# Attention, convolution block and gated block on one core: batch 0 turns its probabilities on TensorE, and the first layer's products stay in PSUM through relu, taps and gate

## The chip, the cores and the metric

The kernel runs on one core of one Trainium2 chip. The metric is device microseconds of that core, the median of three runs: 476.09 us before the change (474.88 to 476.97). Engines are named as the profile names them: PE is TensorE, PEld its weight loads, DVE is VectorE, ACT is ScalarE, POOL is GpSimd, SP is SyncE, which issues all DMAs of this kernel from one queue, in order.

## What is computed

Three layers in a row on 4 batches of 576 positions. The first is causal attention in a window of 128 keys with a linear bias, 8 heads of 64. The second multiplies by `w_in` (512 to 1024), takes relu, forms a gate from 3 taps along the sequence, and multiplies by `w_out` (1024 to 512). The third forms a gate from 5 taps on its input, multiplies the input by `w_val`, gates it and multiplies by `w_out2`.

```python
scores = np.where(mask, scale * q @ k.T + bias, -1e9)
attn = softmax(scores)
x = attn @ v
h = np.maximum(x @ w_in, 0.0)
conv = sum(conv_w[k] * hp[:, k:k + S] for k in range(3))
y = (h * sigmoid(conv)) @ w_out
gate_pre = sum(conv_w2[k] * yp[:, k:k + S] for k in range(5))
out = (sigmoid(gate_pre) * (y @ w_val)) @ w_out2
```

All arrays are float32 in the reference's sense, but the weights and `cw` reach the chip as 64-bit floats and are widened from their two halves on the chip.

## The kernel before, in words

The sequence of each batch is cut into two units, u = 0 (positions 0 to 254, with 256 columns in the first layer) and u = 1 (the rest, with 328 columns). So there are 8 units, (b, u). Each goes through `hidden` (w_in, relu, 3 taps, gate), `mixed` (w_out, 5 taps), `valued` (w_val) and `output` (w_out2). While a unit runs through these four, the attention of the next one is mixed in: four head pairs, each with 4 query blocks of 64 (u = 0) or 5 (u = 1).

The order of all instructions comes from a planner inside the program (`Program.forward` and `backward`): every operation is added with an engine or a choice of engines, an estimated duration, what it reads and writes, and a priority; a list scheduler lays them on the engines, repeats this seven times with priorities from the pass before, and keeps its shortest plan. The engines then run that order, each strictly in its own. Buffers are rings; an operation waits for the last reader of its buffer.

**Attention of one pair** (`attention`): a DMA brings q and k (L502), another v (L505). Scores go to a PSUM bank (`pss`, 3 banks, 2 for the first 20 uses), two blocks to a bank (L541, float32 matmuls). DVE adds the bias and finds the minimum (L545), ACT takes the exponential in place in PSUM with its sum (L549), POOL or DVE and then DVE make the reciprocal `st` (L554, L552, L559). ACT writes the scaled probabilities as float16 to `p` (L575, the high part), DVE the rest (L577, the low part). There is one `p` buffer. When all blocks of a pair are written, SP issues two DMA transposes from `p` to `pt` (L585), one for each part; then PE multiplies by v into `psx` (L617), from where ACT and DVE make the two parts of x (L633, L638, L640).

**Products.** Every weight and every activation is held as a high and a low part, and a product is three matmuls (L657, L658, L659). `dense` takes a bank of the ring `pm` (4 banks, 2 for the first 16 uses, because the widening of the weights uses the other two).

**hidden**, for each of 8 blocks of 128 channels: 12 matmuls into a `pm` bank, then ACT writes the relu to a buffer of ring `t` in SBUF (L692) and so frees the bank. The middle tap goes to a second `t` buffer, on ACT or DVE (L344, L345); two more taps are added by DVE (`fma`, L351), in two of the 8 blocks one of them by ACT and POOL (L361, L362). ACT takes tanh (L702), DVE forms the gate times h (L703, recorded at L351 as `t<-t,t`), and ACT or POOL makes the high part (L335, L337), POOL the low one (L366).

**Weights** (`widen`): a DMA brings a chunk of 512 KB to `raw` (3 buffers, L387), ACT moves its upper word twice (L388 to SBUF, L390 to PSUM), DVE joins the words (L392, L401), ACT or POOL makes the high part (L407, L408), POOL the low part (L366). There are 24 chunks, 8 each of w_in and w_out, 4 each of w_val and w_out2.

**Start.** Until the attention of unit (1, 0), PE is given matmuls on a zero tile wherever its plan is empty (`warm`, L817). DVE instructions that read or write only SBUF, and POOL's, are marked `port=True`: the planner makes them longer where the two run at once.

## Time and profile before

| what | value |
|---|---|
| median of three runs | 476.09 us (474.88 to 476.97) |
| the profiled execution, its own time | 474.43 us |
| its span, first to last instruction | 472.6 us |
| PE, PEld busy (share of the span) | 94%, 88% |
| DVE, ACT, POOL busy | 80%, 71%, 54% |
| mean granted TensorE clock | 0.993 |

Busy times are unions of an engine's instruction records. A matmul record spans its pipeline, so a busy PE is not a PE at its peak. The line after `<-` in a row names what ended the idle time before it. A line number can be that of a helper: L351 is `fma`, L344 and L345 `scaled`, L335 and L337 `cast`, L366 `sub`.

### The profile page before, as it was taken

To read this page: it belongs to the slowest core of one execution; us is meant where nothing else is said; L and a number is where in the kernel's file an instruction comes from. 1 tells how busy PE (TensorE), PEld (TensorE's weight loads), DVE (VectorE), ACT (ScalarE), POOL (GpSimd) and SP (SyncE) were. 2 spreads that over 40 slices of the span, in tenths; PEclk is the share of its full clock that TensorE was granted. 3 is DMA by queue.
4 is the path that set the end of the run, shared out by engine and by line. 5 is a ranking of instruction groups with operands and counts; after the bars stand their busy time and mean duration, and the time that the engine had idled before them with its cause. 6 is when DMAs were issued, how large, how long until landed. Compare 5 with 4: busy or idle time off the path is not lost.

```text
span 472.6 us, 10284 instructions
## 1 busy us (share of the span) xinstructions
PE 446.6 (94%) x3568; PEld 414.0 (88%) x3568; DVE 377.7 (80%) x1009; ACT 334.7 (71%) x964; POOL 256.6 (54%) x379
## 2 busy tenths in 40 slices
PE   7998988879999899999999999999999999999996
PEld 5776876878999899998989899999989999989895
DVE  4688998799898949995999668966999489927690
ACT  3788978898675658785966778765766687846542
POOL 1445987887366607450467447441874167735542
PEclk9999999889999999999999999999999999999999
DMA  8998869699824244646324634666144626640001
GB/s 269 193 235 253 233 149 291 182 236 264 244 59 117 71 118 99 144 102 158 94 47 120 129 94 110 123 145 157 31 98 87 151 64 146 100 101 1 1 0 57
DMA packets 93156, 62.32 MB, mean 132 GB/s; under 512 B 73904, under 2 KB 83888, under 8 KB 93104
## 3 DMA queue, kind: packets, MB, share of 16 engines
q1 hardware_dynamic: 93104, 61.67, 52.4%
q8 instruction: 28, 0.46, 0.4%
q14 instruction: 24, 0.20, 0.1%
HBM read 39.10 MB, written 4.72 MB: 93 GB/s over the span
## 4 chain that ended last, share of the span: by engine, by line
DVE 33%; PE 23%; ACT 9%; issue 6%; POOL 4%; DMA 1%; ACTq 0%; POOLq 0%
DVE t L351 13%; DVE gts L351 10%; PE pm L657 6%; PE pm L658 6%; PE pm L659 6%; PE pss L541 3%; PE psx L617 3%; POOL g L366 2%; DVE p L577 2%; ACT pss L549 2%; DVE pss L545 2%; ACT p L575 1%; ACT t L344 1%; DMA vr<-in_vN 1%; DVE v L351 1%
## 5 line engine op out<-in xcount | busy, mean ns | idle before, releaser
L366 POOL TENSOR_TENSOR g<-t,g 128x254 fp32r<-128x254 f32 (+1 forms) x96 | 85.9, 901 | 18.0 <-ACT g L335 14.2
L351 DVE SCALAR_TENSOR_TENSOR t<-t,cc,t 128x326 f32<-128x326 f32 (+3 forms) x112 | 77.5, 713 | 11.7 <-ACT t L344 10.8
L657 PE MATMUL pm<-g,wout 128*128 128x254 f32 (+1 forms) x256 | 81.1, 317 | 2.0 <-ACT t L344 1.8
L549 ACT ACTIVATE pss<-pss,st 128x192 f32<-128x192 f32 (+2 forms) x144 | 53.9, 374 | 38.0 <-DVE st L545 31.3
L351 DVE SCALAR_TENSOR_TENSOR gts<-t,cc,gts 128x322 f32<-128x322 f32 (+4 forms) x120 | 76.6, 676 | 4.7 <-ACT gts L344 4.0
L657 PE MATMUL pm<-x,win 128*128 128x256 f32 (+1 forms) x256 | 78.7, 307 | 0.0
L658 PE MATMUL pm<-g,wout 128*128 128x254 f32 (+1 forms) x256 | 77.3, 302 | 1.2 <-POOL g L366 1.1
L659 PE MATMUL pm<-g,wout 128*128 128x254 f32 (+1 forms) x256 | 76.8, 300 | 0.8 <-POOL wout L366 0.7
L659 PE MATMUL pm<-x,win 128*128 128x256 f32 (+1 forms) x256 | 76.0, 297 | 0.3 <-POOL win L366 0.3
L658 PE MATMUL pm<-x,win 128*128 128x256 f32 (+1 forms) x256 | 76.2, 298 | 0.0
L541 PE MATMUL pss<-qk 128*128 128x192 f32 (+2 forms) x288 | 57.5, 325 | 7.9 <-DVE p L577 7.8
L554 POOL TENSOR_SCALAR st<-st 128x2 f32<-128x2 f32 (+1 forms) x66 | 16.0, 242 | 85.3 <-ACT pss L549 82.5
L545 DVE CUSTOM_DVE_ANT_0 pss<-pss,bm 128x192 f32<-128x192 f32 (+2 forms) x144 | 47.7, 342 | 14.1 <-PE pss L541 12.6
L337 POOL TENSOR_SCALAR g<-t 128x254 fp32r<-128x254 f32 (+1 forms) x53 | 28.3, 536 | 52.9 <-DVE t L351 36.4
L577 DVE SCALAR_TENSOR_TENSOR p<-pss,st,p 128x192 f16<-128x192 f32 (+2 forms) x139 | 48.8, 387 | 9.8 <-ACT p L575 9.3
L541 PEld LDWEIGHTS pss<-qk 128*128 128x128 f32 x288 | 44.2, 192 | 12.6 <-DVE p L577 11.7
L575 ACT ACTIVATE p<-pss,st 128x192 f16<-128x192 f32 (+2 forms) x139 | 49.2, 404 | 4.8 <-DVE st L559 2.1
L657 PEld LDWEIGHTS pm<-g,wout 128*128 128x128 f32 x256 | 49.0, 191 | 3.6 <-ACT t L344 2.0
L658 PEld LDWEIGHTS pm<-g,wout 128*128 128x128 f32 x256 | 49.3, 193 | 2.0 <-POOL g L366 2.0
L659 PEld LDWEIGHTS pm<-g,wout 128*128 128x128 f32 x256 | 49.3, 193 | 1.2 <-POOL wout L366 1.2
L657 PEld LDWEIGHTS pm<-x,win 128*128 128x128 f32 x256 | 48.3, 189 | 1.5 <-issue 0.9
L659 PEld LDWEIGHTS pm<-x,win 128*128 128x128 f32 x256 | 48.2, 188 | 0.5 <-POOL win L366 0.5
(100 smaller groups left out, 1169.9 us busy)
## 6 DMA issues: line engine op xcount, KB each, us to landing
qk<-in_qk SPq DMA_DIRECT2D x16, 544.0 KB, 4.1
qk<-in_qk SPq DMA_DIRECT2D x16, 384.0 KB, 3.8
raw<-in_w_out SPq DMA_DIRECT2D x12, 512.0 KB, 4.2
raw<-in_w_in SPq DMA_DIRECT2D x8, 512.0 KB, 5.4
vr<-in_vN SPq DMA_DIRECT2D x16, 256.0 KB, 2.9
raw<-in_vN SPq DMA_DIRECT2D x8, 384.0 KB, 3.8
out<-t SPq DMA_DIRECT2D x16, 161.0 KB, 1.9
raw<-in_w_val SPq DMA_DIRECT2D x4, 512.0 KB, 3.9
```

The costliest lines, as they stand in the source:

```text
L337: "POOL": (pool_t(n), lambda: nc.gpsimd.tensor_scalar(hi, src, 1.0, 0.0, op0=ALU.mult, op1=ALU.add))}
L351: pg.add("DVE", dve_t(n, 0 if isinstance(scalar, float) else 1), lambda: nc.vector.scalar_tensor_tensor(out=out, in0=in0, scalar=scalar, i ...
L366: "POOL": (pool_t(n, True), lambda: nc.gpsimd.tensor_tensor(out=lo, in0=src, in1=hi.bitcast(F32), op=ALU.subtract))}
L541: return [nc.tensor.matmul(out=o, lhsT=q_t[:, i, :], rhs=k_t[:, kc:kc + nkey], start=True, stop=True, skip_group_check=True) for i, o, nke ...
L545: pg.add("DVE", 128 + 1.05 * nkey, lambda i=i, s=s, nkey=nkey: nc.vector.tensor_tensor_reduce(out=s, in0=s, in1=bm[:, p, 192 - nkey:192], ...
L549: pg.add("ACT", act_t(nkey, True, 2), lambda i=i, s=s: nc.scalar.activation(out=s, in_=s, func=AF.Exp, scale=-1.0, bias=stt[:, 0, i:i + 1] ...
L554: "POOL": (165, lambda a=a, e=e: nc.gpsimd.tensor_scalar(stt[:, 2, a:e], stt[:, 1, a:e], 1e-9, 1.0 / PSC, op0=ALU.add, op1=ALU.mult))}
L575: pg.add("ACT", act_t(nkey, True, 1), lambda i=i, s=s, hi=hi: nc.scalar.activation(out=hi, in_=s, func=AF.Copy, scale=stt[:, 2, i:i + 1]), ...
L577: pg.add("DVE", dve_t(nkey, 1), lambda i=i, s=s, hi=hi, lo=lo: nc.vector.scalar_tensor_tensor(out=lo, in0=s, scalar=stt[:, 2, i:i + 1], in ...
L657: return [nc.tensor.matmul(out=o, lhsT=wh, rhs=hi, start=first, stop=False), nc.tensor.matmul(out=o, lhsT=wh, rhs=lo, start=False, stop=Fa ...
L658: nc.tensor.matmul(out=o, lhsT=wh, rhs=lo, start=False, stop=False),
L659: nc.tensor.matmul(out=o, lhsT=wl, rhs=hi, start=False, stop=last)]
```

## The change

In batch 0 (`b < TURN`), ACT writes the exponential unscaled, as float32, to the `p` buffer, which holds the same bytes seen as 10 x 128 floats. For each query block a diagonal matrix `dg` = identity times the reciprocal is made by DVE or POOL (ring of 3). PE multiplies: the probabilities are the stationary operand, `dg` the moving one, so that PSUM receives the transposed and scaled probabilities, in the bank that held the scores. There are 64 such matmuls of 128 columns: 6 for a pair of u = 0, 10 for one of u = 1. ACT copies them as float16 to `pt` (high part), DVE subtracts for the low part, one instruction each for a group of one or two query blocks. The 16 DMA transposes of batch 0 are gone; batches 1 to 3 are as before. The zeroes in `p` are set again for float16 before batch 1.

In `hidden`, in all batches, the relu is written in place in the `pm` bank. The middle tap, the other two and the gate read it there, so the bank is released by the gate and not by the relu. Ring `t` has 9 buffers in place of 10. The planner's cost of a transfer is scaled by 1.17 and not by 1.3, and that of a transposed block goes from 142 to 162 before scaling, which leaves a transpose where it was and makes other transfers cheaper in its eyes.

```diff
+TURN = 1
...
-    ring_t = Ring("t", 10, [128, XMAX], F32)
+    ring_t = Ring("t", 9, [128, XMAX], F32)
...
+    ring_dg = Ring("dg", 3, [128, 128], F32)
...
-        return pg.add("SP", issue, fn, prio, reads, writes, 0.0, xfer * 1.3)
+        return pg.add("SP", issue, fn, prio, reads, writes, 0.0, xfer * 1.17)
...
+        turn = b < TURN
+        pe_ = pb.rearrange("p q a c -> p (q a c)").bitcast(F32)
...
+                if turn:
+                    c0 = 256 * i + 128 * (j0 + i < 2) + 64 * ((j0 + i) % 2 and j0 + i > 1)
+                    to, tok = pe_[:, c0:c0 + nkey], ((pk, 0, i),)
...
+                    pg.add(("DVE", "POOL"), (dve_t(128, 1, True), pool_t(128, False, 1)), (
+                        lambda dg=dg, ri=ri: nc.vector.tensor_scalar(dg, eye, ri, None, op0=ALU.mult),
+                        lambda dg=dg, ri=ri: nc.gpsimd.tensor_scalar(dg, eye, ri, 0.0, op0=ALU.mult, op1=ALU.add)),
+                        pr, ((stk, 2, gi), "eye"), (dk,), port=True)
...
+                        return [nc.tensor.matmul(out=gp[:, 128 * (x - 2 * a):128 * (x - 2 * a) + 128], lhsT=pe_[:, 128 * x:128 * x + 128],
+                                                 rhs=dg, start=True, stop=True, skip_group_check=True) for x in sl]
+                    pg.add("PE", len(sl) * mm4_t(128), rows, pr, ((pk, 0, i), dk), ((sk, 0), (sk, 1)))
...
+                pg.add("ACT", act_t(128 * sn, True), lambda src=src, hi=hi: nc.scalar.activation(out=hi, in_=src, func=AF.Copy),
+                       pr, ((sk, 0), (sk, 1)), ((ptk, 0, gi),), bank=sk)
+                pg.add("DVE", dve_t(128 * sn), lambda src=src, hi=hi, lo=lo: nc.vector.tensor_tensor(
+                    out=lo, in0=src, in1=hi, op=ALU.subtract), pr, ((sk, 0), (sk, 1), (ptk, 0, gi)), ((ptk, 1, gi),), bank=sk)
+                continue
...
-        for q in range(2):
+        for q in range(0 if turn else 2):
...
-            h, hk2 = ring_t.next()
...
+            h = hp
+            pg.add("ACT", act_t(Nx, True), lambda h=h: nc.scalar.activation(out=h[:, 0:Nx], in_=h[:, 0:Nx], func=AF.Relu),
+                   pr, (), (hk,), bank=hk)
+            scaled(c, h[:, d:d + Ng], c1[:, m, 1:2], Ng, pr, (hk, "cc"), (ak,), ('ACT', 'DVE'), True, hk)
...
-            fma(c, c, 1.0, h[:, d:d + Ng], ALU.add, ALU.mult, Ng, pr, (hk2,), (ak,))
+            fma(c, c, 1.0, h[:, d:d + Ng], ALU.add, ALU.mult, Ng, pr, (hk,), (ak,), hk)
```

How the order moves is shown at three places. The first is SP's queue near the start, from the first chunk of w_in on (`raw` receives weights, `qk` queries and keys, `vr` values). Before:

```order
L387 DMA raw1_75<-in_w_in 128x1024
L502 DMA qk0_106<-in_qk0 128x768
L585 DMA_TRANSPOSE pt0_117<-p0_116 128x7x128 x2
L387 DMA raw0_74<-in_cw 128x88
L387 DMA raw2_76<-in_w_in 128x1024
L502 DMA qk1_107<-in_qk0 128x768
L585 DMA_TRANSPOSE pt1_118<-p0_116 128x7x128 x2
L387 DMA raw0_74<-in_w_in 128x1024
L502 DMA qk0_106<-in_qk1 128x1088
L585 DMA_TRANSPOSE pt0_117<-p0_116 128x7x128 x2
L387 DMA raw1_75<-in_w_in 128x1024
```

Now:

```order
L389 DMA raw1_75<-in_w_in 128x1024
L389 DMA raw0_74<-in_cw 128x88
L389 DMA raw2_76<-in_w_in 128x1024
L504 DMA qk0_105<-in_qk0 128x768
L507 DMA vr0_107<-in_vN 128x512
L504 DMA qk1_106<-in_qk0 128x768
L389 DMA raw0_74<-in_w_in 128x1024
L389 DMA raw1_75<-in_w_in 128x1024
L389 DMA raw2_76<-in_w_in 128x1024
L504 DMA qk0_105<-in_qk1 128x1088
```

No load stands behind a transpose any more until batch 1; loads wait for free buffers alone.

The second place is PE at the second pair of unit (0, 0) (`pss0` and `pss1` are score banks). Before, the scores of the second pair follow zero matmuls, and nothing but scores is in the banks:

```order
L541 MATMUL pss0_123<-qk1_107 128x64
L541 MATMUL pss0_123<-qk1_107 128x128
L817 LDWEIGHTS idle_73
L817 MATMUL pss2_125<-idle_73 128x256
L817 LDWEIGHTS idle_73
```

Now the turned probabilities of the first pair are made just ahead of these scores:

```order
L585 MATMUL pss1_126<-dg2_118,p0_115 128x128 x2
L585 MATMUL pss1_126<-dg0_116,p0_115 128x128 x2
L547 MATMUL pss0_125<-qk1_106 128x64
L547 MATMUL pss0_125<-qk1_106 128x128
L858 LDWEIGHTS idle_73
```

Six matmuls with `dg` have come in for this pair (two for its first bank stand further up). In the whole program the zero matmuls go from 284 to 173.

The third place is DVE in `hidden` of unit (0, 1) (`t` are SBUF buffers, `pm` PSUM banks, `cc` the taps). Before:

```order
L351 SCALAR_TENSOR_TENSOR t5_100<-t4_99,cc_69,t5_100 128x326
L345 TENSOR_SCALAR t7_102<-t6_101,cc_69 128x326
L351 SCALAR_TENSOR_TENSOR t5_100<-t4_99,cc_69,t5_100 128x325
L351 SCALAR_TENSOR_TENSOR t7_102<-t6_101,cc_69,t7_102 128x326
L351 SCALAR_TENSOR_TENSOR t5_100<-t5_100,t4_99 128x326
```

Now:

```order
L353 SCALAR_TENSOR_TENSOR t0_95<-pm3_124,cc_69,t0_95 128x326
L353 SCALAR_TENSOR_TENSOR t8_103<-pm2_123,cc_69,t8_103 128x325
L353 SCALAR_TENSOR_TENSOR t0_95<-pm3_124,cc_69,t0_95 128x325
L551 ISA pss1_126,st1_114<-pss1_126,bm_72 128x64
L551 ISA st1_114 128x1
L353 SCALAR_TENSOR_TENSOR t8_103<-t8_103,pm2_123 128x326
```

One of the two wide operands of every tap and gate is now a PSUM bank. In the whole program DVE's middle taps of `hidden` (L345, now L347) go from 13 to 25.

## Rows read from the trace of the kernel before

**Rows 1.** Stretches: length, busy PE, PEld, DVE, ACT, POOL, clock, DMA share, GB/s.
```profile
0.00:40.00 40.00, 33.81 (x273) 26.09 (x273) 27.41 (x98) 28.15 (x87) 15.33 (x35) 1.00 0.93 232
40.00:80.00 40.00, 36.22 (x313) 31.12 (x313) 38.18 (x96) 34.63 (x92) 31.90 (x42) 1.00 0.80 232
80.00:118.00 38.00, 31.84 (x256) 29.09 (x255) 34.00 (x87) 33.62 (x92) 31.62 (x39) 0.91 0.84 227
118.00:472.00 354.00, 344.78 (x2733) 327.73 (x2731) 278.14 (x731) 238.29 (x699) 177.71 (x264) 1.00 0.42 99
```

**Rows 2.** PE's waits from 118 to 472 us: total, times, longest.
```profile
PE pm L658 <- POOL g L366: 3.4, 7, 0.8
```

**Rows 3.** Stretches with two transposes and little else, columns as in rows 1.
```profile
150.50:153.50 3.00, 2.86 (x25) 2.56 (x24) 2.96 (x3) 1.81 (x5) 3.00 (x4) 1.00 0.82 153
194.40:198.00 3.60, 3.60 (x30) 3.60 (x29) 3.60 (x6) 1.99 (x5) 2.25 (x4) 1.00 0.99 182
```

**Rows 4.** SP's timeline: the fourth pair's transposes, the last w_in chunk.
```profile
31.70 2.72 SPq L585 DMA_TRANSPOSE pt<-p  x2
...
38.88 0.33 SPq L387 DMA_DIRECT2D raw<-in_w_in  x1
```

**Rows 5.** PE's timeline: PE begins w_in in earnest; later one run of scores.
```profile
40.35 0.38 PE L657 MATMUL pm<-x,win 128*128 128x256 f32 x1
...
221.99 2.01 PE L541 MATMUL pss<-qk 128*128 128x192 f32 x12
```

**Rows 6.** DVE's groups by shape, 0 to 118 us: count, busy us, mean ns, idle.
```profile
L392 DVE SCALAR_TENSOR_TENSOR pm<-pm,sg 128x512 uint32<-128x512 uint32 x24 | 16.8, 699 | 3.2 <-ACT pm L390 3.0
...
L577 DVE SCALAR_TENSOR_TENSOR p<-pss,st,p 128x192 f16<-128x192 f32 x31 | 11.5, 408 | 0.2
...
L351 DVE SCALAR_TENSOR_TENSOR t<-t,t 128x254 f32<-128x254 f32 x8 | 6.5, 823 | 0.0
...
L351 DVE SCALAR_TENSOR_TENSOR t<-t,cc,t 128x254 f32<-128x254 f32 x8 | 6.2, 793 | 0.0
L351 DVE SCALAR_TENSOR_TENSOR t<-t,cc,t 128x253 f32<-128x253 f32 x6 | 4.3, 709 | 0.0
...
L742 DVE SCALAR_TENSOR_TENSOR gts<-gts,pm 128x254 f32<-128x254 f32 x4 | 1.6, 404 | 0.0
...
L345 DVE TENSOR_SCALAR t<-t,cc 128x254 f32<-128x254 f32 x1 | 0.3, 334 | 0.0
```

**Rows 7.** DVE's timeline: a tap, then two gates one after the other.
```profile
62.28 0.47 DVE L351 SCALAR_TENSOR_TENSOR t<-t,cc,t 128x254 f32<-128x254 f32 x1
...
62.95 0.41 DVE L351 SCALAR_TENSOR_TENSOR t<-t,t 128x254 f32<-128x254 f32 x1
...
63.36 1.42 DVE L351 SCALAR_TENSOR_TENSOR t<-t,t 128x254 f32<-128x254 f32 x1
```

**Rows 8.** ACT's and POOL's groups by shape, 0 to 118 us, columns as in rows 6.
```profile
L390 ACT ACTIVATE pm<-raw 128x512 f32<-128x512 f32 x24 | 15.4, 641 | 0.0
...
L575 ACT ACTIVATE p<-pss,st 128x192 f16<-128x192 f32 x31 | 11.6, 419 | 0.9 <-DVE st L559 0.8
...
L337 POOL TENSOR_SCALAR g<-t 128x254 fp32r<-128x254 f32 x7 | 3.3, 478 | 0.4 <-DVE t L351 0.4
```

**Rows 9.** Timelines, hidden of unit (0, 1): first and fourth relu, their gates, a matmul.
```profile
121.75 0.45 ACT L692 ACTIVATE t<-pm 128x328 f32<-128x328 f32 x1 [2.06 <-PE pm L659]
...
126.94 0.43 ACT L692 ACTIVATE t<-pm 128x328 f32<-128x328 f32 x1
...
124.91 0.95 DVE L351 SCALAR_TENSOR_TENSOR t<-t,t 128x326 f32<-128x326 f32 x1
...
133.03 0.49 DVE L351 SCALAR_TENSOR_TENSOR t<-t,t 128x326 f32<-128x326 f32 x1
...
126.26 0.32 PE L658 MATMUL pm<-x,win 128*128 128x328 f32 x1
126.42 0.31 PE L659 MATMUL pm<-x,win 128*128 128x328 f32 x1
```

More of the change, by code (lines that the diff above doesn't have):

```diff
@@ L339, in cast, with scaled @@
         pg.add(use, tuple(engs[e][0] for e in use), tuple(engs[e][1] for e in use), prio, reads, writes, port=True)
-    def scaled(out, in_, scale, n, prio, reads, writes, engs, psum=False):
+    def scaled(out, in_, scale, n, prio, reads, writes, engs, psum=False, bank=None):
         ap = 0 if isinstance(scale, float) else 1
@@ L347, in scaled, with fma, tap @@
         pg.add(tuple(engs), tuple(how[e][0] for e in engs), tuple(how[e][1] for e in engs), prio, reads, writes,
-               port=not psum)
-    def fma(out, in0, scalar, in1, op0, op1, n, prio, reads, writes):
+               bank=bank, port=not psum)
+    def fma(out, in0, scalar, in1, op0, op1, n, prio, reads, writes, bank=None):
         pg.add("DVE", dve_t(n, 0 if isinstance(scalar, float) else 1), lambda: nc.vector.scalar_tensor_tensor(
-            out=out, in0=in0, scalar=scalar, in1=in1, op0=op0, op1=op1), prio, reads, writes, port=True)
-    def tap(out, in0, w, n, prio, reads, key, shared):
+            out=out, in0=in0, scalar=scalar, in1=in1, op0=op0, op1=op1), prio, reads, writes, bank=bank, port=bank is None)
+    def tap(out, in0, w, n, prio, reads, key, shared, bank=None):
         if not shared:
-            fma(out, in0, w, out, ALU.mult, ALU.add, n, prio, reads, (key,))
+            fma(out, in0, w, out, ALU.mult, ALU.add, n, prio, reads, (key,), bank)
             return
@@ L360, in tap @@
         t = t[:, 0:in0.shape[1]]
-        pg.add("ACT", act_t(n, False, 1), lambda: nc.scalar.activation(out=t, in_=in0, func=AF.Copy, scale=w), prio, reads, (tk,))
+        pg.add("ACT", act_t(n, bank is not None, 1), lambda: nc.scalar.activation(out=t, in_=in0, func=AF.Copy, scale=w), prio, reads, (tk,), bank=bank)
         pg.add("POOL", pool_t(n, True), lambda: nc.gpsimd.tensor_tensor(out=out, in0=out, in1=t, op=ALU.add), prio, (tk,), (key,))
@@ L580, in attention @@
         ca, ce = (1, 8) if u == 0 else (0, 10)
-        pt, ptk = ring_pt.next()
         pr = prio + step * nb
-        for q in range(2):
+        if not turn:
+            pt, ptk = ring_pt.next()
+        for q in range(0 if turn else 2):
             src = pb[:, q, ca:ce, :].rearrange("p a c -> p (a c)")
             sync(lambda q=q, src=src: nc.sync.dma_start_transpose(out=pt[:, q, ca:ce, :], in_=src),
-                 pr, tuple((pk, q, i) for i in range(nb)), ((ptk, q),), (ce - ca) * 142.0, 650.0)
+                 pr, tuple((pk, q, i) for i in range(nb)), tuple((ptk, q, gi) for gi in range(3)), (ce - ca) * 162.0, 650.0)
         if u == 0:
@@ L624, in attention @@
             dur = sum(64 * m[5] * m[7] / 2.4 + 27 for _, m in ms if m[-1] == 0) + 7
-            rd = tuple((ptk, q) for q in sorted({g[0] for g in gr})) + tuple((vk, q + 1) for q in sorted({g[1] for g in gr}))
+            rd = tuple((ptk, q, gi) for q in sorted({g[0] for g in gr}) for gi in range(len(groups))) + tuple((vk, q + 1) for q in sorted({g[1] for g in gr}))
             pg.add("PE", dur, lambda ms=ms: do_pv(ms), pr, rd, (xpk,)).drain = True
@@ L691, in hidden @@
             c = a[:, 0:Ng]
-            how = {"ACT": (act_t(Nx, True), lambda h=h, hp=hp: nc.scalar.activation(out=h[:, 0:Nx], in_=hp[:, 0:Nx], func=AF.Relu)),
-                   "DVE": (dve_t(Nx), lambda h=h, hp=hp: nc.vector.tensor_scalar(h[:, 0:Nx], hp[:, 0:Nx], 0.0, None, op0=ALU.max))}
-            use = ('ACT',)
-            pg.add(use, tuple(how[x][0] for x in use), tuple(how[x][1] for x in use), pr, (hk,), (hk2,))
-            scaled(c, h[:, d:d + Ng], c1[:, m, 1:2], Ng, pr, (hk2, "cc"), (ak,), ('ACT', 'DVE'))
+            h = hp
+            pg.add("ACT", act_t(Nx, True), lambda h=h: nc.scalar.activation(out=h[:, 0:Nx], in_=h[:, 0:Nx], func=AF.Relu),
+                   pr, (), (hk,), bank=hk)
+            scaled(c, h[:, d:d + Ng], c1[:, m, 1:2], Ng, pr, (hk, "cc"), (ak,), ('ACT', 'DVE'), True, hk)
             for i, k in enumerate((0, 2)):
@@ L810, in attention_moe_moe_kernel @@
             if u2 == 0:
+                if b2 == TURN:
+                    zeros(False, base)
                 prepare(b2, base - 10000)
```

38 lines of the change are left out of this document (28 added, 10 removed).

## The prediction, made before the changed kernel was run

> **What bounds the kernel now.** I read the table of stretches first, then PE's waits, then the queue, the groups of DVE and the timeline of one `hidden` stage.
>
> The stretches [rows 1] show two regimes. From 118 us on PE is busy 344.8 of 354 us, while DVE has 278.1, ACT 238.3 and the DMA share is 0.42. The waits that the view can name there are small: the longest entry for PE is 3.4 us, on POOL's low part of an activation [rows 2]. So after 118 us time goes only if PE is given less to do, and what can be won from waits is a few us. Before 118 us it is different. In the first 40 us the DMA share is 0.93, DVE is busy 27.4 us and ACT 28.2 us: the chip is waiting for data and for the attention's chain. From 40 to 118 us DVE is busy 38.2 + 34.0 = 72.2 of 78 us, 93%, with ACT at 34.6 + 33.6 = 68.2 us: the vector work of widening, attention and `hidden` sets the pace. PE is not the bound there: 284 of its matmuls are the zero ones, all before 118 us. So I cost the change as: how much earlier does PE get into its saturated stretch, and what does it then find changed.
>
> **Start, 0 to 40 us.** A pair of transposes of u = 0 takes 0.82 x 3.0 = 2.5 us of all DMA engines, one of u = 1 0.99 x 3.6 = 3.6 us [rows 3]. The four pairs of unit (0, 0) are thus 9.8 of the 37 us of DMA work in this stretch. They are also obstacles in SP's queue: the fourth pair's is issued at 31.70 us and the last chunk of w_in at 38.88 us [rows 4], and PE begins the run of w_in at 40.35 us [rows 5]. In the new order no load stands behind one. The gain lies between 0, if the attention's chain on DVE and ACT sets the 40 us anyway, and 9.8 us. In the chain the transposes' landing is replaced by a diagonal, two to four matmuls, a copy and a subtraction. I take 7 us, nearer the upper end, because DVE is idle 12.6 us and ACT 11.8 us of these 40.
>
> **DVE, 40 to 118 us.** Removed: 36 low parts of batch 0 at 0.408 us for 192 columns [rows 6] (28 of them, and 8 shorter ones, estimated at 0.31), 13.9 us. Added: 12 subtractions over 512 columns, at most 0.699 us as the widening's PSUM instruction of that width, and 8 over 256 at 0.404 us as the gating of `valued` [rows 6], 11.6 us; and 13 diagonals of 128 columns, at about 0.334 us, the middle tap from SBUF [rows 6], 4.3 us. That is +2.0 us. In `hidden` of unit (0, 0) the 8 gates took 0.823 us and the 14 taps 0.793 and 0.709 us: 6.6 + 6.3 + 4.3 = 17.2 us [rows 6]. They are long because something holds them: the same gate takes 0.41 us once and 1.42 us right after, a tap 0.47 us [rows 7]. An instruction with one operand in PSUM, L742, has a mean of 0.404 us [rows 6]. From PSUM I take 0.404 for a gate and 0.47 for a tap: 9.8 us, a gain of 7.4. Three more middle taps go to DVE, 3 x 0.47 = 1.4 us. Sum -4.0 us, and at 93% busy -4.3 us of time. The bounds are +3.7 us (no gain from PSUM) and -7 us (subtractions and diagonals at half the price, the held instructions' neighbours freed too).
>
> **What is covered.** ACT loses 36 high parts, 28 x 0.419 and 8 estimated at 0.33, 14.4 us, and gains 12 copies at 0.641 at most and 8 estimated at 0.37 [rows 8], 10.7 us; DVE, the busier one, covers it. POOL gets 23 diagonals at no more than 0.478 us [rows 8], up to 11 us, on an engine that is busy 63.5 of 78 us; it fits, but if POOL became late the low parts of w_out2 would be late with it. PE gets 64 matmuls: six float32 ones of 192 columns take 2.01 us [rows 5], so one of 128 columns about 0.22 us, 14 us in all. Their cover is the plan's empty places, where the zero matmuls go from 284 to 173; with that cover gone they cost all 14 us. The 14.2 us of DMA time of unit (0, 1)'s transposes is covered too, since DVE binds then. Ring `t` with 9 buffers costs nothing: `hidden` now takes one buffer for a block in place of two. The planner's new transfer costs only move loads. At the end of unit (0, 0) the new order has done less of the next attentions: one pair's 30 products with v and 6 blocks of scores remain, 3 us that PE then pays.
>
> **After 118 us.** The taps and gates of the seven other `hidden` stages get shorter in the same way; DVE is not the bound, so of this only waits like POOL's 3.4 us [rows 2] can come back. I take 2 us, between 0 and 6. Against it stands the PSUM bank, now held until the gate. In unit (0, 1) the first relu starts at 121.75 us and its gate ends at 125.86 us, 4.1 us; the fourth starts at 126.94 and its gate ends at 133.52, 6.6 us [rows 9]. A block of 12 matmuls at 0.15 us [rows 9] takes 1.8 us, four banks 7.2 us. A bank's round is then 1.8 for the products, about 0.4 to the relu and 4.1 to 6.6 more: 6.3 to 8.8 us, so a block waits for 0 to 1.6 us. Two taps and a gate that lose some 0.2 us each bring 6.6 down to 6, and other work in the order (attention) can stand in the gap. I take 0, between 0 and 1.6 us for each of some 20 rounds. In unit (0, 0) only two banks serve 8 blocks, four rounds of 1.4 + 0.4 + about 6 us: 31 us, while DVE needs as long for its share there; I take 0.
>
> **Sum.** -7 - 4.3 + 3 - 2 = -10.3 us. The profiled execution took 474.4 us (span 472.6), which makes 464.1; the median of the runs is 1.7 us above that execution, so I forecast **466 us**.
>
> **A rule against the change.** The rows say that a wide DVE instruction with one operand in PSUM has no long cases [rows 6, 7]. The Trainium skill, VectorE: DVE Perf Modes, section Rules for kernel authors, advises for elementwise work on a matmul's output to accept the slowest rate or to copy it to SBUF first if many operations follow. That is what the kernel did before, and by this page the change goes the wrong way; for the taps and gates this case's rows disagree, for the single-operand middle tap no row decides.
>
> **Rivals.**
> 1. *The start opens wide*, 456 us: the full 9.8 us there, the 7 us of DVE, 6 us of waits, less 3, gives -20. For it: two engines idle for 30% of the start. Against it: DVE is then at once the limit. Chance 0.13.
> 2. *The transposes were hidden anyway*, 473 us: the chain of scores, minimum, exponential and reciprocal sets the start, so the 7 us fall away and -3.3 remain. For it: unit (0, 0) uses one `p` buffer and two score banks, which are now held for the matmul, copy and subtraction too. Chance 0.18.
> 3. *The PSUM bank becomes the wait*, 480 us, slower. In each of the seven later `hidden` stages PE stands before the fifth to eighth block, and `mixed` before its first, until the gate four blocks earlier. The price is 8 to 34 us (7 stages, some 3 rounds, 0.4 to 1.6 us); at 2 us for a stage and the rest of the sum kept at half, since the stalls begin in unit (0, 0), it is 476 - 10 + 14 = 480. It decides from a lag of 5 us between relu and gate (7.2 - 1.8 - 0.4), which the rows straddle. For it: 6.6 us. Against it: 4.1 us, and shorter DVE work. Chance 0.16.
> 4. *Reading PSUM is no cheaper for DVE*, 474 us: the held instructions are slow for another reason, so -4.3 becomes +3.7 and -2 stays: -2.3 us. For it: the low part L577, which reads PSUM with a scalar from SBUF, takes 0.408 us for only 192 columns [rows 6]. Against it: L742's 0.404 us for 254. This is where the page's advice would be right. Chance 0.07.
>
> **How the numbers follow.** The forecast has 0.46 and spans 461 to 471 us. The range is to hold 8 in 10: forecast (0.46), rivals 2 and 4 (0.25), half of rival 1 and a part of rival 3: 457 to 478 us. A measurement here can tell 0.5%, 2.4 us, from no change: faster means below 473.7, slower above 478.5. Faster: the forecast almost whole (0.45), rival 1 (0.13), half of rival 2 and of rival 4 (0.12): 0.70. Slower: most of rival 3, 0.15. The same: 0.15.
>
> **What would show it.** In the new profile the run of w_in on PE should begin near 33 us and the last output of unit (0, 0) be computed near 108 us, not 118. The groups of DVE should show `t<-pm,cc,t` at 0.45 to 0.58 us and `t<-t,pm` at 0.40 to 0.50 us; 0.7 or more would mean rival 4. The DMA share of the first 40 us should fall below 0.9 or the same loads land sooner. PE's waits after the start should stay below 6 us for each cause; a large entry with a gate of `hidden` (`t<-t,pm`) as the releaser of a `pm` matmul is rival 3. The forecast is wrong if w_in still begins at 40 us, or if a unit of the saturated part takes longer than before.

## The result, and the profile after

The changed kernel takes **460.0 us** (458.5 to 460.7) against 476.5 us (474.9 to 477.2) of the kernel before, measured side by side: a ratio of 0.965, 95% interval 0.962 to 0.968. That is 16.5 us faster where 10 were forecast. The sign is right, and the time lies inside the range of 457 to 478 us. It lies below the 461 to 471 us that the forecast itself was to span, nearer to the 456 us of rival 1 than to 466. The way there was in part another than the one I had worked out.

The profiled execution of the changed kernel took 460.6 us, with a span of 458.8 us. Its table of stretches, cut as in [rows 1] (length, busy PE, PEld, DVE, ACT, POOL, granted clock, DMA share, GB/s):

```profile
0.00:40.00 40.00, 34.58 (x272) 28.08 (x273) 30.62 (x95) 28.36 (x78) 24.81 (x49) 1.00 0.77 256
40.00:80.00 40.00, 38.14 (x325) 33.40 (x324) 37.21 (x100) 38.83 (x100) 34.09 (x48) 1.00 0.59 202
80.00:118.00 38.00, 36.20 (x304) 33.39 (x303) 33.87 (x85) 26.69 (x73) 24.35 (x40) 1.00 0.59 171
118.00:458.00 340.00, 335.63 (x2691) 321.54 (x2690) 250.12 (x741) 230.05 (x690) 164.54 (x267) 1.00 0.44 97
```

Three things differ from before. The DMA share of the start fell from 0.93 to 0.77 while more bytes per second arrived (256 against 232 GB/s). From 80 to 118 us PE is busy 36.2 us where it was 31.8 (1.7 us of that on zero matmuls, which have gone from this stretch). And the granted clock of that third stretch is 1.00, where it was 0.91. From 118 us on DVE is busy 74% of the time (79% before) and POOL 48% (50%).

Where the time was won is read from PE's timeline: when the last product of each stage of unit (0, 0) starts. These are the rows of the changed kernel for the start of the run of w_in, the end of `hidden` and the end of the output:

```profile
40.31 0.36 PE L693 MATMUL pm<-x,win 128*128 128x256 f32 x1
...
67.47 0.28 PE L695 MATMUL pm<-x,win 128*128 128x256 f32 x1
...
108.07 0.28 PE L695 MATMUL pm<-g,wo 128*128 128x254 f32 x1
```

With the same rows of both kernels for the other stages (in us):

| last product of | before | after | difference |
|---|---|---|---|
| attention, unit (0, 0) (p x v) | 37.0 | 38.5 | +1.5 |
| `hidden` | 57.4 | 67.5 | +10.1 |
| `mixed` | 95.5 | 85.9 | -9.6 |
| `valued` | 109.0 | 97.5 | -11.6 |
| output of unit (0, 0) | 118.2 | 108.1 | -10.1 |
| output of the last unit | 468.6 | 455.1 | -13.5 |

So nothing is won by 40 us; `hidden` even ends later. All of the first 10 us are won between the end of `hidden` and the end of the output, and 3.3 us more in the seven later units.

SP's queue shows what ran ahead. The last six of the eight chunks of w_in now go out in two runs with no transpose between them, and the last chunk of any weight goes out at 79.97 us. In the kernel before it went out at 104.65 us:

```profile
15.78 3.67 SPq L389 DMA_DIRECT2D raw<-in_w_in  x3
...
24.12 5.99 SPq L389 DMA_DIRECT2D raw<-in_w_in  x3
...
32.02 5.88 SPq L389 DMA_DIRECT2D raw<-in_w_out  x3
...
79.97 0.33 SPq L389 DMA_DIRECT2D raw<-in_w_out  x1
```

(`in_w_out` at 79.97 us is w_out2; the view cuts the name's last digit.) The fourth pair's transposes stood in this queue at 31.70 us and the last chunk of w_in at 38.88 us [rows 4]; now chunks of w_out go out from 32.02 us.

DVE's groups up to 104 us, about the end of `valued` (count, busy us, mean ns, idle before):

```profile
L593 DVE TENSOR_TENSOR pt<-pss,pt 128x512 f16<-128x512 f32 x12 | 8.2, 680 | 0.4 <-ACT pt L591 0.4
L577 DVE TENSOR_SCALAR dg<-eye,st 128x128 f32<-128x128 f32 x13 | 6.4, 492 | 0.1
...
L353 DVE SCALAR_TENSOR_TENSOR t<-pm,cc,t 128x254 f32<-128x254 f32 x8 | 3.8, 469 | 0.0
L353 DVE SCALAR_TENSOR_TENSOR t<-t,pm 128x254 f32<-128x254 f32 x8 | 3.3, 411 | 0.4 <-ACT t L736 0.3
L593 DVE TENSOR_TENSOR pt<-pss,pt 128x256 f16<-128x256 f32 x7 | 2.9, 416 | 0.1
...
L353 DVE SCALAR_TENSOR_TENSOR t<-pm,cc,t 128x253 f32<-128x253 f32 x6 | 2.8, 468 | 0.0
...
L347 DVE TENSOR_SCALAR t<-pm,cc 128x254 f32<-128x254 f32 x4 | 1.9, 474 | 0.6 <-ACT pm L728 0.6
```

The gates cost 0.411 us where they cost 0.823, the taps 0.469 where they cost 0.793 and 0.709 [rows 6]. And PE's waits from 118 us on (total, times, longest), all that are over 0.1 us:

```profile
PE pm L694 <- POOL g L368: 0.7, 3, 0.3
PE pm L693 <- ACT t L346: 0.3, 1, 0.3
PE pm L693 <- DVE t L353: 0.2, 1, 0.2
PE psx L653 <- DMA pt<-p: 0.2, 1, 0.2
```

POOL's 3.4 us [rows 2] are 0.7. A gate of `hidden` (DVE, `t`, L353) as releaser of a PSUM bank stands there with 0.2 us.

### The profile page after: what moved, and what is told of

Its sections match the earlier page's. It is cut to its first block, busy times and chain, and to the rows that moved or that the text cites. A ratio compares the mean times of both kernels' runs of the same rounds, so it can differ in the third digit from the quotient of the medians.

```text
span 458.8 us, 10275 instructions
## 1 busy us (share of the span) xinstructions
PE 444.5 (97%) x3585; PEld 416.4 (91%) x3585; DVE 351.8 (77%) x1019; ACT 323.9 (71%) x938; POOL 247.8 (54%) x402
## 4 chain that ended last, share of the span: by engine, by line
PE 43%; DVE 18%; ACT 13%; DMA 9%; POOL 6%; issue 3%; SPq 0%; ACTq 0%; POOLq 0%; DVEq 0%
PE pm L693 12%; PE pm L694 12%; PE pm L695 11%; DVE gts L353 7%; PE pss L547 4%; PE psx L653 4%; DMA pt<-p 3%; DMA raw<-in_w_out 3%; DVE t L353 2%; POOL g L368 2%; DMA vr<-in_vN 2%; ACT pss L559 2%; ACT p L610 1%; ACT sg L390 1%; ACT t L346 1%
## 5 line engine op out<-in xcount | busy, mean ns | idle before, releaser
L368 POOL TENSOR_TENSOR g<-t,g 128x254 fp32r<-128x254 f32 (+1 forms) x96 | 80.7, 842 | 25.5 <-ACT g L337 21.1
L353 DVE SCALAR_TENSOR_TENSOR gts<-t,cc,gts 128x322 f32<-128x322 f32 (+4 forms) x120 | 78.4, 682 | 10.4 <-ACT gts L346 8.7
L693 PE MATMUL pm<-g,wout 128*128 128x254 f32 (+1 forms) x256 | 79.7, 311 | 0.0
L694 PE MATMUL pm<-g,wout 128*128 128x254 f32 (+1 forms) x256 | 76.2, 298 | 0.0
L695 PE MATMUL pm<-g,wout 128*128 128x254 f32 (+1 forms) x256 | 75.8, 296 | 0.0
L353 DVE SCALAR_TENSOR_TENSOR t<-pm,cc,t 128x325 f32<-128x325 f32 (+3 forms) x112 | 56.0, 513 | 11.6 <-ACT t L346 9.0
L339 POOL TENSOR_SCALAR g<-t 128x254 fp32r<-128x254 f32 (+1 forms) x55 | 26.1, 474 | 69.0 <-DVE t L353 34.1
L693 PEld LDWEIGHTS pm<-x,win 128*128 128x128 f32 x256 | 48.2, 188 | 4.4 <-DVE t L353 2.3
L559 ACT ACTIVATE pss<-pss,st 128x192 f32<-128x192 f32 (+2 forms) x108 | 40.6, 376 | 15.3 <-DVE st L551 14.0
L693 PEld LDWEIGHTS pm<-g,wout 128*128 128x128 f32 x256 | 48.2, 188 | 1.4 <-DVE t L353 0.3
L612 DVE SCALAR_TENSOR_TENSOR p<-pss,st,p 128x192 f16<-128x192 f32 (+2 forms) x103 | 36.5, 386 | 16.1 <-DMA pt<-p 10.8
L694 PEld LDWEIGHTS pm<-x,win 128*128 128x128 f32 x256 | 48.3, 189 | 0.4 <-DVE x L676 0.4
L695 PEld LDWEIGHTS pm<-g,wout 128*128 128x128 f32 x256 | 48.6, 190 | 0.0
L694 PEld LDWEIGHTS pm<-g,wout 128*128 128x128 f32 x256 | 48.5, 190 | 0.0
L695 PEld LDWEIGHTS pm<-x,win 128*128 128x128 f32 x256 | 48.2, 188 | 0.0
L346 ACT ACTIVATE t<-pm 128x254 f32<-128x254 f32 (+2 forms) x64 | 25.8, 409 | 26.9 <-PE pm L695 26.9
```

The lines of the kernel that those rows point to most:

```text
L339: "POOL": (pool_t(n), lambda: nc.gpsimd.tensor_scalar(hi, src, 1.0, 0.0, op0=ALU.mult, op1=ALU.add))}
L346: how = {"ACT": (act_t(n, psum, ap), lambda: nc.scalar.activation(out=out, in_=in_, func=AF.Copy, scale=scale)), "DVE": (dve_t(n, ap, fast ...
L353: pg.add("DVE", dve_t(n, 0 if isinstance(scalar, float) else 1), lambda: nc.vector.scalar_tensor_tensor(out=out, in0=in0, scalar=scalar, i ...
L368: "POOL": (pool_t(n, True), lambda: nc.gpsimd.tensor_tensor(out=lo, in0=src, in1=hi.bitcast(F32), op=ALU.subtract))}
L559: pg.add("ACT", act_t(nkey, True, 2), lambda i=i, s=s, to=to: nc.scalar.activation(out=to, in_=s, func=AF.Exp, scale=-1.0, bias=stt[:, 0, ...
L612: pg.add("DVE", dve_t(nkey, 1), lambda i=i, s=s, hi=hi, lo=lo: nc.vector.scalar_tensor_tensor(out=lo, in0=s, scalar=stt[:, 2, i:i + 1], in ...
```

## The experiments

Theory: the transposes' place in the queue and on the DMA engines holds up the weights, and DVE's work on the copies in SBUF is long because something holds it; the planner's new costs and the shorter ring are worth nothing. Rivals: the new costs do part of it; the transposes were hidden; the parts need each other; another order of the planner, whatever the reason for it, moves the time by itself.

Experiments 1 to 4, 5 to 8 and 9 to 12 were each measured beside the kernel before, which took 476.1, 475.8 and 475.3 us there. The differences below are of medians in us; taken by the ratios to the kernel before, some come out about 1 us larger.

**1. The planner's costs alone.** The kernel before, with the two new figures:

```diff
-        return pg.add("SP", issue, fn, prio, reads, writes, 0.0, xfer * 1.3)
+        return pg.add("SP", issue, fn, prio, reads, writes, 0.0, xfer * 1.17)
...
-                 pr, tuple((pk, q, i) for i in range(nb)), ((ptk, q),), (ce - ca) * 142.0, 650.0)
+                 pr, tuple((pk, q, i) for i in range(nb)), ((ptk, q),), (ce - ca) * 162.0, 650.0)
```

> Only the planner's two costs of transfers are changed (1.17 and 162); attention and hidden are as before. Theory (the time came from the loads that no longer stand behind transposes, and from DVE's shorter taps): the order moves a little, 474 to 479 us. Rival (the new costs let the planner issue loads sooner, and that is the gain): below 470 us.

Measured: 471.3 us (ratio 0.989, 0.986 to 0.993), 4.8 us faster, between the two expectations. I had costed this at nothing and missed. In its trace the last chunk of a weight goes out at 99 us (before: 105), and the output of unit (0, 0) starts its last product at 113.7 us (118.2). The order that the planner writes for the same work is better, and it is another order throughout: only about four in ten of DVE's instructions keep their place in the sequence. Which of the two figures does it stays open; they weren't tried apart.

**2. The turn alone.** The changed kernel with `hidden` copied to SBUF by relu and worked on there, as before, with nine buffers of `t`:

```diff
+            h, hk2 = ring_t.next()
...
-            h = hp
...
-            fma(c, c, 1.0, h[:, d:d + Ng], ALU.add, ALU.mult, Ng, pr, (hk,), (ak,), hk)
+            fma(c, c, 1.0, h[:, d:d + Ng], ALU.add, ALU.mult, Ng, pr, (hk2,), (ak,))
```

> Batch 0 turns its probabilities on TensorE, hidden works in SBUF as before (ring t has 9 buffers, since the diagonals need the room). Theory: the weights arrive early as in the changed kernel (last load issued near 80 us), but DVE keeps its 7 us of long taps before 100 us and more later: 466 to 470 us. Rival (PSUM taps are the whole gain): 474 to 480 us. Rival (the turn is the whole gain): 459 to 462 us.

Measured: 472.2 us (0.991, 0.989 to 0.994), outside all three expectations. It is no better than the costs alone, which it contains, so by this run the turn is worth nothing, or something in this kernel takes the gain away. Experiment 9 looks for it.

**3. PSUM alone.** The changed kernel with `TURN = 0`: batch 0 goes through DMA transposes, the costs are the new ones.

> Hidden works in PSUM in all batches, batch 0 uses DMA transposes as before. Theory: DVE is 7 us shorter before 118 us and 25 us over the program, the loads stay behind the transposes: 466 to 472 us. Rival (the turn is the whole gain): 474 to 479 us. Rival (PSUM taps are the whole gain): 459 to 462 us.

Measured: 466.7 us (0.980, 0.978 to 0.982), as expected. Against experiment 1, `hidden` in PSUM is worth 4.6 us; against the changed kernel, the turn is worth 6.7 us. Its trace has DMA shares of 0.94 and 0.89 in the first two stretches of 40 us, and the clock of 80 to 110 us is 0.94.

**4. The old costs.** The changed kernel with the diff of experiment 1 taken back: 1.3 and 142.

> The changed kernel with the planner's former costs of transfers (1.3 and 142). Theory: within 2 us of the changed kernel, 458 to 462 us. Rival (the costs matter): above 465 us.

Measured: 462.4 us (0.973, 0.969 to 0.976), between the two expectations. On top of both parts the new costs are worth 2.4 us, half of what they are worth alone.

**5 and 6. How much is the luck of an order?** The planner may write another order after any small change. The same edit, an issue cost of 470 in place of 475, was made in the kernel before and in the changed one:

```diff
-    def sync(fn, prio, reads=(), writes=(), xfer=0.0, issue=475.0):
+    def sync(fn, prio, reads=(), writes=(), xfer=0.0, issue=470.0):
```

> The kernel before, with nothing changed but the planner's figure for issuing a DMA, 470 for 475 ns. It measures how far the time moves when the planner merely lays another order. Theory (the costs of transfers matter by what they say): within 2 us of the kernel before. Rival (any new order moves the time by several us, and the 5 us of the run with the costs alone is such a throw): more than 3 us off, either way.

> The changed kernel with the same small figure, 470 for 475 ns. Theory: within 2 us of the changed kernel (458 to 462 us). Rival (new orders scatter): more than 3 us off, and then single parts of the change can't be told apart to better than that.

Measured: 475.6 us (1.000, 0.998 to 1.002) and 458.5 us (0.964, 0.961 to 0.967). The first is no change, the second 1.5 us below the changed kernel, with intervals that overlap. But the question stays open, because the order hardly moved. In the traces the kernel of experiment 5 runs the same instructions in the same order as the kernel before on every engine (1009 on DVE, 964 on ACT, 195 DMAs on SP), and that of experiment 6 differs from the changed kernel only in the place of one DMA. So 0.2 and 1.5 us are what nearly the same order moves from one measurement to another. In the other experiments the planner wrote another order, as in experiment 1, and how much of each difference is the luck of that order was not tested. The differences of 2 to 3 us (experiments 4, 7 and 8) are the least certain. 458.5 us is the lowest time of the study; it isn't told apart from the changed kernel's.

**7 and 8. The transposes put back, for nobody.** Experiment 7 is the changed kernel with seven buffers of `t`, which makes room. Experiment 8 adds to it, for batch 0, two DMA transposes for a pair into a tile that nobody reads. They stand in SP's queue behind the turned probabilities; for u = 0 they cover five of the seven blocks. As both write the one spare tile, each waits for the one before to land.

```diff
-    ring_t = Ring("t", 9, [128, XMAX], F32)
+    ring_t = Ring("t", 7, [128, XMAX], F32)
+    spare = st("spare", [128, 10, 128], F16)
...
+        for q in range(2 if turn else 0):
+            c3 = 3 if u == 0 else ca
+            src = pt[:, q, c3:ce, :].rearrange("p a c -> p (a c)")
+            sync(lambda src=src, c3=c3: nc.sync.dma_start_transpose(out=spare[:, c3:ce, :], in_=src),
+                 pr, tuple((ptk, q, gi) for gi in range(len(groups))), ("spare",), (ce - ca) * 162.0, 650.0)
```

> The changed kernel with 7 buffers in ring t in place of 9, as a base for the next run, which needs the room. Theory: hidden uses one buffer for a block, so 7 do: 459 to 463 us.

> As the run with 7 buffers, but 16 DMA transposes of batch 0 are put back into the queue: from pt to a spare tile of which nobody reads, at the place where they stood. Products and results stay those of TensorE's turn. Theory (much of the turn's gain is that loads of weights don't stand behind transposes, and the 24 us of DMA time): 4 to 9 us slower than with 7 buffers alone, weights landing 10 us later or more. Rival (the gain is in DVE's and ACT's instructions): within 2 us.

Measured: 463.0 us (0.974, 0.970 to 0.978) and 466.1 us (0.980, 0.976 to 0.983). Two buffers fewer cost 3.0 us. The idle transposes cost 3.1 us more. The first two stretches of 40 us, of experiment 7:

```profile
0.00:40.00 40.00, 33.99 (x265) 26.46 (x266) 31.12 (x97) 27.81 (x76) 21.26 (x44) 1.00 0.73 247
40.00:80.00 40.00, 38.13 (x326) 33.99 (x324) 38.63 (x105) 38.05 (x97) 34.36 (x53) 1.00 0.60 189
```

and of experiment 8:

```profile
0.00:40.00 40.00, 33.78 (x263) 26.97 (x264) 30.54 (x93) 26.34 (x72) 20.06 (x43) 1.00 0.89 250
40.00:80.00 40.00, 37.49 (x305) 32.80 (x303) 38.11 (x105) 36.45 (x94) 33.81 (x50) 1.00 0.89 237
```

The DMA share is back to near that of before, and yet only 3.1 of the turn's 6.7 us are gone, less than the 4 to 9 us expected. The weights were not held up as they had been: the last chunk goes out at 91.8 us against 89.1 in experiment 7, 2.7 us later where 10 or more were expected. So the 3.1 us price the DMA time, and little of what it costs that weights stand behind transposes.

Experiment 3, where batch 0 uses its transposes, tells what else the turn took away. PE's waits up to 118 us there (total, times, longest):

```profile
PE pm L695 <- POOL wval L368: 3.9, 2, 2.1
PE psx L653 <- DMA pt<-p: 3.4, 3, 1.9
```

The first is for the low part of w_val, which POOL has ready at 99.2 us there and at 84.8 us in the changed kernel. The second is for the landing of a transpose. The changed kernel has neither. How the two and the DMA time divide the 6.7 us, no run tells.

**9. The ring alone.** Experiment 1 with nine buffers of `t`:

```diff
-    ring_t = Ring("t", 10, [128, XMAX], F32)
+    ring_t = Ring("t", 9, [128, XMAX], F32)
```

> The kernel before with the two new transfer costs (e1_costs_alone, 471.3 us) and ring t cut from 10 to 9 buffers, nothing else. With the hidden units still copied to SBUF, a block takes two buffers of t, so 9 hold four blocks and a half. Theory (the ring is what held the turn alone back): 474 to 478 us, 3 to 6 us over e1_costs_alone, and the units after the first longer. Rival (the ring is free): within 1.5 us of e1_costs_alone, 470 to 473 us; then the turn alone truly brings nothing while hidden stays in SBUF.

Measured: 478.3 us (1.005, 1.002 to 1.008), 7.0 us over experiment 1 and just above the theory's 474 to 478. So the shorter ring accounts for experiment 2: against 478.3, the turn alone is worth 6.1 us, close to the 6.7 us on top of PSUM. The two comparisons rest on different orders, which speaks for the size. What the ring costs is less sure: of 9.5 us between the profiled executions of experiments 9 and 1, 6.3 lie in one unit, (2, 0), around one wait of PE (the last section has it). In order: the costs -4.8, the ring +7.0, the turn -6.1, PSUM -12.2 us; or, with PSUM ahead, the costs -4.8, PSUM and the shorter ring -4.6, the turn -6.7 us. `hidden` in PSUM takes one buffer of `t` for a block in place of two, and by this sum more than half of its 12.2 us is that it does without the tenth buffer.

**10. One bank fewer.** The changed kernel with three banks of `pm` from the second half of unit (0, 0) on:

```diff
-    ps_m.spare = (16, 16)
+    ps_m.spare = (16, 10**9)
```

> The changed kernel with three banks of pm in place of four from the second half of unit (0,0) on (two before that, as now). A bank's round in hidden is 1.8 us of products, 0.4 to the relu and 4 to 6 us to the gate, 6.2 to 8.2 us; three banks are 5.4 us of PE's work. Theory (the bank's hold is near to being the wait, four banks just cover it): 0.8 to 2.8 us for some 19 rounds in seven stages, 470 to 490 us, and PE's waits on the gate as releaser of a pm matmul grow to over 8 us. Rival (other work in the order fills the gap, or the planner places around it): under 465 us.

Measured: 468.0 us (0.985, 0.981 to 0.989), 8.0 us slower than with four. That is between the two expectations, nearer to the theory. The wait that rival 3 described appears, first of PE's waits from 108 us on, though with 4.3 us and not over 8:

```profile
PE pm L693 <- DVE t L353: 4.3, 8, 1.1
```

With four banks it is 0.2 us. The mechanism is real, and the fourth bank covers it; these waits name 4.3 of the 8.0 us.

**11. The turn in two batches.** The changed kernel with `TURN = 2`.

> The changed kernel with the turn in batches 0 and 1, so 64 more matmuls of about 0.22 us on TensorE, 14 us, where no zero matmuls stand beside them. Theory (their cover was the start's empty places): units (1,0) and (1,1) together 10 to 15 us longer, 469 to 475 us. Rival (they replace waits for the transposes' landing, or PE's time there is not the bound): 458 to 464 us. The transposes' 16 us of DMA time of batch 1 go away in both.

Measured: 475.0 us (0.998, 0.996 to 1.001). That is 15.0 us over the changed kernel and eats the whole gain. By PE's timeline units (0, 1), (1, 0) and (1, 1) are 4.6 us longer, 10.3 longer and 2.2 shorter than there: 12.8 us in all, not all in the two units that I had named, as the attention of batch 1 is computed partly ahead of its own units. Another 2.0 us lie in unit (0, 0), where no matmul was added. PE from 110 us on is busy 99.7%:

```profile
110.00:458.00 348.00, 347.09 (x2829) 333.75 (x2829) 258.45 (x763) 231.84 (x681) 169.70 (x278) 1.00 0.37 89
```

My price of 14 us for 64 matmuls without cover nearly holds. In batch 0 zero matmuls made room: up to 118 us they keep PE busy 23.7 us in the changed kernel and 32.6 us in experiment 3.

**12. A third bank at the start.** The changed kernel with three banks of `pm` for the first 16 takings; the third is also used by the widening:

```diff
-    ps_m.spare = (16, 16)
+    ps_m.spare = (16,)
```

> The changed kernel with three banks of pm in place of two for the first 16 takings (hidden and mixed of unit (0,0)); the third is shared with the widening of the weights. Theory (two banks held until the gate are why hidden of unit (0,0) now ends at 67 us and not 57): it ends 4 to 8 us earlier, and the whole is 0 to 3 us faster, 457 to 460 us, as the DVE work up to 108 us stays the same. Rival (the order of DVE's work, not the bank, sets it, and the widening loses a bank): hidden ends at 66 us or later and the whole is 460 to 466 us.

Measured: 473.7 us (0.996, 0.994 to 0.998), 13.7 us slower, worse than either side expected. `hidden` of unit (0, 0) ends at 91.2 us and not at 67.5. Blocks of `hidden` and the widening of weights now share a bank, and it is `hidden` that falls behind: the last chunk of a weight goes out at 74.8 us (80.0 in the changed kernel). So the two-bank limit there can't be tested by taking one from the widening. The other traces tell which part of the change makes `hidden` end late there: it ends between 53 and 58 us in the kernel before and in experiments 1, 2, 5 and 9, which copy it to SBUF, and between 64 and 69 us in the changed kernel and in experiments 3, 4, 6, 7, 8, 10 and 11, which keep it in PSUM, whether they turn or not.

## Why the prediction was right, and where it was not

**The start, -7 us: the step failed as put.** The prediction said that "the run of w_in on PE should begin near 33 us", since no load stands behind a transpose. It begins at 40.31 us (40.35 before [rows 5]) and the attention of unit (0, 0) ends 1.5 us later. That was one of the prediction's own signs of being wrong ("if w_in still begins at 40 us"). For the first 40 us rival 2's account fits better: the chain of scores, minimum, exponential and reciprocal sets the pace, and the two score banks are now held for the turn as well. The weights came earlier without PE starting earlier: the last low part of w_in is ready at 39.8 us (52.7 before). PE's timeline of the changed kernel shows scores waiting for a bank until the subtraction is done, 1.3 us in all up to 40 us:

```profile
24.44 0.71 PE L547 MATMUL pss<-qk 128*128 128x64 f32 x4 [0.81 <-DVE pt L593]
...
30.43 0.92 PE L547 MATMUL pss<-qk 128*128 128x192 f32 x4 [0.30 <-DVE pt L593]
```

What rival 2 had wrong is the conclusion that nothing is then won. In the meantime the weights ran ahead, their last chunk goes out 25 us earlier, and from 80 to 118 us PE has 1.8 us of gaps and not 6.2. For the kernel before, the longest entry that the view of waits names for PE there is on ACT, and the second row tells for what: ACT copies a finished bank of `mixed` to SBUF, late, as it also widens weights.

```profile
PE pm L657 <- ACT t L344: 2.9, 2, 1.8
86.90 0.63 ACT L344 ACTIVATE t<-pm 128x254 f32<-128x254 f32 x2
```

With the rest of the change in place, the turn took away PE's waits for the low part of w_val and for transposes to land (3.9 and 3.4 us, experiment 8). With all that hangs on it, it was worth 6.1 to 6.7 us (experiments 3 and 9). The size of the term was nearly right; the place was not.

**DVE up to 118 us, -4.3 us: the durations hold, the time they were to save there does not.** Experiments 1 and 3 differ in `hidden` (and one buffer of `t`). The output of unit (0, 0) starts its last product at 113.7 us in the one and at 113.8 in the other: nothing is won up to there. What `hidden` in PSUM wins comes later, below. The sum was also laid on 40 to 118 us whole, though 19 of the 36 low parts that it takes away start before 40 us.

To the durations. Gates and taps of unit (0, 0) take 3.8 + 3.3 + 2.8 = 9.9 us where 9.8 were forecast. The subtractions take 8.2 + 2.9 = 11.1 us (at most 11.6; one short one is later than 104 us). The diagonals are the one miss: 0.492 us each and not 0.334, 6.4 us and not 4.3. Rival 4 fell. The Trainium skill, VectorE: DVE Perf Modes, section Rules for kernel authors, advises a copy to SBUF if many operations follow; here two taps and a gate follow, and each is faster from PSUM, 0.41 and 0.47 us against 0.82 and 0.79 us. For the middle tap, with one wide operand, the advice is right: 0.474 us for 254 columns from PSUM, 0.334 from SBUF (a single case, [rows 6]). In the changed kernel the taps of `mixed` still work on SBUF and still take 0.714 us for 322 columns, while `hidden`'s from PSUM take 0.551 us for 325 (rows from 104 us on):

```profile
L353 DVE SCALAR_TENSOR_TENSOR gts<-t,cc,gts 128x322 f32<-128x322 f32 x60 | 40.7, 714 | 8.1 <-ACT gts L346 7.7
...
L353 DVE SCALAR_TENSOR_TENSOR t<-pm,cc,t 128x325 f32<-128x325 f32 x32 | 17.5, 551 | 1.6 <-POOL t L364 1.5
L353 DVE SCALAR_TENSOR_TENSOR t<-t,pm 128x326 f32<-128x326 f32 x32 | 15.5, 487 | 1.9 <-ACT t L736 1.7
```

The Trainium skill, SBUF — State Buffer, section SBUF: two separate sides, says that a DVE instruction with two SBUF inputs and a GpSimd one that reads SBUF lock each other out for a whole instruction. The traces agree. The 1.42 us gate of [rows 7], begun at 63.36 us, lies beside this instruction of POOL:

```profile
63.10 1.40 POOL L366 TENSOR_TENSOR wout<-gts,wout 128x512 fp32r<-128x512 f32 x1 [0.73 <-ACT wout L407]
```

Of the 32 gates of 326 columns in the kernel before, 10 ran while POOL was idle and took at most 0.495 us; the other 22 took up to 1.186 us. In the changed kernel, with one operand in PSUM, 11 ran while POOL was idle and 21 beside it, and none took over 0.496 us. Of all 296 taps and gates with two wide SBUF operands in the kernel before, 124 are more than 0.06 us longer than their shape takes with POOL idle, and POOL was at work during each of them. So PSUM is not the faster source; it keeps the instruction out of POOL's way. No run took POOL's work away as a test.

**The planner's costs: the term that was left out.** "The planner's new transfer costs only move loads", I wrote, at nothing. They were worth 4.8 us alone and 2.4 us on top of the rest. The loads do go out sooner (the last chunk at 99 us and not at 105), but the new figures moved every engine's order, and whether the loads, the rest of the order or its luck is the gain isn't shown.

**The ring.** "Ring `t` with 9 buffers costs nothing" was not measured for the whole change, where `hidden` takes one buffer for a block. While `hidden` is copied to SBUF, taking the tenth buffer away costs 7.0 us (experiment 9), and two buffers fewer cost 3.0 us even now (experiment 7).

**Leftover attention, +3 us.** Unit (0, 1) is 54.9 us long and was 52.3: +2.6, the size that was forecast. By PE's timeline 30 products with v and 6 blocks of scores are left over, as counted. But experiment 3, which leaves nothing over, has 54.2 us there, so that the leftover is the cause isn't shown. (A longer unit in the saturated part was to be a sign that the forecast is wrong; this one was in its sum.)

**After 118 us, -2 us: too small.** From the output of unit (0, 0) to that of the last unit it was 350.3 us and is 347.0, with the 2.6 us in it: about 6 us won, the upper end of the bounds. Experiment 1, without PSUM, has 351.6 us there, experiment 3, with it, 345.9. This is where `hidden` in PSUM won its time: 5.7 us.

**The PSUM hold, 0 us.** Right for the later units: rival 3's wait is 0.2 us, and takes one bank fewer to appear (experiment 10). In unit (0, 0), where I took 0 for two banks, `hidden` ends 10.1 us later, in every kernel that keeps it in PSUM (experiment 12). The stages behind it win more than that, and what the late end costs is open.

**The price of the 64 matmuls without cover** was put at 14 us; experiment 11 measured 15.0, of which 12.8 lie in the units concerned.

**The clock, which the prediction didn't speak of.** [Rows 1] had it: 0.91 from 80 to 118 us, that is 38 x 0.09 = 3.4 us of TensorE's full speed lost. The changed kernel has 1.00 there, and experiments 2, 4, 7 and 8, which turn, have 1.00 from 80 to 110 us. The last section has the rows.

**The sum.** Forecast: start -7 with +3 for what is left over, DVE and waits -6.3, costs 0. Measured, by runs: the turn -6.7, PSUM with the shorter ring -4.6, the costs -4.8, which make the 16 us. The traces (one execution each) tell where, by the start of the last product of an output:

| us | costs (before to 1) | PSUM, nine buffers (1 to 3) | turn (3 to changed) | sum |
|---|---|---|---|---|
| up to the output of unit (0, 0) | -4.5 | +0.1 | -5.7 | -10.1 |
| from there to the last output | +1.2 | -5.7 | +1.1 | -3.3 |

Up to the output of unit (0, 0) the forecast had -7 - 4.3 = -11.3 us, and "near 108 us" for it came out at 108.1. That is partly luck: the -4.3 us didn't come there, and the planner's costs, put at nothing, filled their place. Behind it the forecast had +1 us and -3.3 were measured. So the sign and the range were right for three gains of about 5 us each, of which the prediction had one at its size (the turn, by another path), one in the wrong place (PSUM) and one not at all (the costs).

## What to carry to other kernels

A transfer that is taken off a shared queue need not help the stage that it belonged to; ask which loads then run ahead and which later stage was waiting for them. A planner's cost figures are part of a change, and a buffer that a change saves can be worth as much as the work it saves: try each by itself on both kernels before one is costed at nothing. Where orders are written by a program, compare them before a run is taken as a sample of another order. Work given to TensorE is covered only where its timeline has fillers or gaps: the turn gained 6 to 7 us in batch 0, and the same 64 matmuls in batch 1 lost 15 us.
